# Eight-expert MoE behind an FFT filter: weight halves written once to DRAM, scales from sums of squares, float16 from a later group

## The chip, the core and the metric

The kernel runs on one core of a Trainium2 chip. The time is the device time of one execution, in microseconds (us); three executions of the kernel before give a median of 2247.62 us (2238.39 to 2249.82).

## What is computed

A filter in the frequency domain over the 2496 positions of 8 batches, and then a mixture of experts: each of the 19968 rows goes to the two of 8 experts with the highest noisy logits.

```python
X = np.fft.rfft(x, axis=1)                      # x: 8 x 2496 x 256
y = np.fft.irfft(X * (filt_r + 1j * filt_i), n=2496, axis=1)
x = y.reshape(19968, 256)
noisy = x @ w_gate + np.log1p(np.exp(x @ w_noise)) * noise
top2 = np.argpartition(-noisy, 2, axis=1)[:, :2]      # weights: softmax over the two
for e in range(8):
    for k in range(2):
        mask = top2[:, k] == e
        out[mask] += top2_w[mask, k, None] * (np.maximum(x[mask] @ w1[e], 0) @ w2[e])
# w1: 8 x 256 x 1024, w2: 8 x 1024 x 256
```

## The kernel before

**Two streams, one order.** `fft_stream` (L611) yields the filter step by step: short Fourier transforms as matmuls (`s1`, `kgl` to `kg2`, `t3`, `i2`), rows `y` written to DRAM with their gate values, then gating and routing of a finished batch, which fill `tabs` (the expert of each block) and `lst` (its rows). `expert` (L1242) is a second stream, over blocks of up to 512 routed rows of one expert. `run` (L1315) interleaves the two: a block yields 13 times, and after each yield `run` takes as many filter steps as `PACE` allows for the group. A scheduler then sets the order within each engine from the written program, save where `pin` holds a step at its place.

**Blocks.** They come in groups by how many batches are routed ("ready"). With ready 1 to 3 there are 2, 10 and 6 single blocks of 512 rows. From ready 4 to 8 two blocks of one expert share its weights: 3 pairs with ready 4, then four groups of 5 pairs. Behind them stand the rows left over: 7 single blocks of 512, 14 units of 256 rows and 4 of 128, and more units in a branch (`tc.If`) that the data of this run don't need.

**One block.** POOL gathers the rows (`gather`, L1079), a DMA transposes them (`flip`, L1118) and `turn` splits them into a high and a low half. `front` (L1056) loads the weights (`load_w`, L1186) and splits them (`wsplit`, L1212), 4 pieces of w1 and 4 of w2, one ACT instruction for the high half and one DVE instruction for the low half each. Every product is made of three matmuls, high by high, high by low and low by high (`_mm3`, L123; its matmuls have the lines 124 to 126 wherever it is called from `expert`). A block has 8 `hps` tiles of 6 matmuls, 48 of 128x512, each tile followed by ACT's Relu `hh` (L1278) and DVE's `hl` (L1279), and 96 `yps` matmuls of 128x256. ACT scales `yps` by the gate into `stage` (L1305), POOL adds it to `out` in DRAM (L1306).

**Two number formats.** With `ready < HALF` the halves are float32 of reduced mantissa (in the rows: f32). With `ready >= HALF`, here 4, they are float16 (f16), scaled by powers of two: for the rows by the greatest |y| of the batches (`ymax`, a DVE reduction of each filter output in `i2`, L544), for the weights by the greatest |w| of each expert. The latter is found by `wscales` (L582): 64 loads `wp` of 256 KB on SP's queue, 64 DVE reductions (L593), then `powers` and the table `wtab` (L608). It is a generator, `self.preps`, whose next step is written at every second `write()`, a call that each filter step of the later batches makes. At the first block with `ready >= HALF`, `gather` writes all steps that are left, and then POOL copies the block's scales into `sc` (L1090).

**Weights of the units.** A block or pair of 512 rows loads its 8 pieces into slots of `stage`. A unit loads w1 as 1 MB into `wb` (tag G) and w2 by turns into `stage` slots or into `wc`. Every unit splits what it has loaded. `fetch` keeps two blocks ahead, of which one may stand transposed.

## Time and profile before

| | |
|---|---|
| median of 3 runs | 2247.62 us |
| the profiled execution, by its own time | 2256.64 us |
| its span in the profile | 2254.8 us |
| mean granted TensorE clock | 0.982 |
| PE busy | 2132.7 us (95%) |
| DVE busy | 1594.0 us (71%) |
| ACT busy | 1327.7 us (59%) |
| POOL busy | 1040.2 us (46%) |
| DMA | 392.37 MB, mean 174 GB/s |

PE is TensorE's matmuls, PEld its weight loads, which run beside them; DVE, ACT and POOL are VectorE, ScalarE and GpSimd, SP is the engine that only issues DMAs. A row of a group of instructions reads: line, engine, operation, out<-in by the program's names, partitions x elements and type, count, busy time and mean time of one in ns, and behind the last bar the idle time ahead of them with what ended it. The mean of a matmul is from its start to its end, and these overlap; the pace of a row of matmuls is read from their starts.

### The profile page before, as it was taken

The numbers are of one execution on the slowest core, as the hardware profiler recorded it, in microseconds if no ns is written. First come the engines' busy times: TensorE is split into PE (matmuls) and PEld (weight loads), VectorE is DVE, ScalarE is ACT, GpSimd is POOL, SyncE is SP. The second block draws the span as 40 slices with busy tenths as digits, with TensorE's granted clock in tenths as the row PEclk, the third lists the DMA queues.
The fourth block names the chain that finished last, engine by engine and source line by source line (L and its number), as shares of the span: only waits on it lengthen the run. The fifth ranks groups of instructions, "written<-read, shape, count | busy, mean of one in ns | idle before, by whom it ended". The sixth has DMA issues, their size and how long they took to land. (4 is left out here: it accounts for less than half of the span.)

```text
span 2254.8 us, 43746 instructions
## 1 busy us (share of the span) xinstructions
PE 2132.7 (95%) x14522; PEld 1564.4 (69%) x14522; DVE 1594.0 (71%) x3463; ACT 1327.7 (59%) x2513; POOL 1040.2 (46%) x955
## 2 busy tenths in 40 slices
...
GB/s 239 160 239 174 233 209 176 218 217 215 186 186 200 175 148 179 179 159 157 170 149 152 133 146 131 175 120 132 118 127 136 120 124 141 175 175 245 247 251 146
DMA packets 485871, 392.37 MB, mean 174 GB/s; under 512 B 206251, under 2 KB 387587, under 8 KB 485635
## 3 DMA queue, kind: packets, MB, share of 16 engines
...
q14 instruction: 120, 0.98, 0.2%
...
## 5 line engine op out<-in xcount | busy, mean ns | idle before, releaser
L124 PE MATMUL yps<-w,hh 128*128 128x256 f16 (+1 forms) x2528 | 686.9, 277 | 13.9 <-ACT hh L1278 8.7
L125 PE MATMUL yps<-w,hh 128*128 128x256 f16 (+1 forms) x2528 | 679.9, 276 | 0.1
L126 PE MATMUL yps<-w,hl 128*128 128x256 f16 (+1 forms) x2528 | 670.7, 276 | 7.6 <-DVE hl L1279 6.1
L1306 POOL DMA_INDIRECT out<-stage,ids x316 | 529.5, 1676 | 312.4 <-ACT stage L1305 222.8
L1094 POOL DMA_INDIRECT stage<-y,ids x316 | 352.9, 1117 | 556.7 <-DMA xt<-stage 470.6
L1279 DVE SCALAR_TENSOR_TENSOR hl<-hps,hh 128x512 f16<-128x512 f32 (+3 forms) x712 | 429.2, 621 | 215.1 <-ACT hh L1278 163.6
L124 PE MATMUL hps<-mxh,w1h 128*128 128x512 f16 (+3 forms) x1424 | 497.4, 362 | 18.1 <-DVE hl L1279 13.2
L125 PE MATMUL hps<-mxl,w1h 128*128 128x512 f16 (+3 forms) x1424 | 507.3, 360 | 1.6 <-DVE mxl L1176 1.3
L126 PE MATMUL hps<-mxh,w1l 128*128 128x512 f16 (+3 forms) x1424 | 505.8, 359 | 0.0
L1278 ACT ACTIVATE hh<-hps 128x512 f16<-128x512 f32 (+3 forms) x712 | 373.0, 548 | 143.5 <-PE hps L126 135.7
L1305 ACT ACTIVATE stage<-yps,gt 128x256 f32<-128x256 f32 x316 | 143.6, 476 | 327.4 <-PE yps L126 167.7
L124 PEld LDWEIGHTS <-hh 128*128 128x128 f16 x1952 | 191.2, 98 | 63.7 <-ACT hh L1278 7.8
L126 PEld LDWEIGHTS <-hl 128*128 128x128 f16 x1952 | 190.3, 98 | 63.6 <-DVE hl L1279 13.4
L125 PEld LDWEIGHTS <-hh 128*128 128x128 f16 x1952 | 191.2, 98 | 43.2 <-issue 6.0
L126 PEld LDWEIGHTS <-w1l 128*128 128x128 f16 x1136 | 111.4, 98 | 100.3 <-issue 1.2
L125 PEld LDWEIGHTS <-w1h 128*128 128x128 f16 x1136 | 111.5, 98 | 87.9 <-issue 17.9
L124 PEld LDWEIGHTS <-w1h 128*128 128x128 f16 x1136 | 111.4, 98 | 71.1 <-issue 7.4
L1134 DVE SCALAR_TENSOR_TENSOR w1l<-stage,sc,w1h 128x512 f16<-128x512 f32 x120 | 88.8, 744 | 77.3 <-ACT w1h L1133 50.6
L540 ACT COPY yt<-q 117x1024 uint16<-117x1024 uint16 x96 | 90.6, 944 | 52.5 <-PE q L534 41.9
L1228 DVE SCALAR_TENSOR_TENSOR w<-stage,sc,w 128x512 f16<-128x512 f32 x156 | 111.9, 744 | 9.3 <-ACT w L1227 3.8
L124 PEld LDWEIGHTS yps<-w,hh 128*128 128x128 f32 x576 | 110.3, 192 | 11.2 <-ACT hh L1278 4.1
L1133 ACT ACTIVATE w1h<-stage,sc 128x512 f16<-128x512 f32 x120 | 86.0, 719 | 50.0 <-PE hps L125 29.3
...
## 6 DMA issues: line engine op xcount, KB each, us to landing
...
```

The lines of the kernel that those rows point to most:

```text
L124: nc.tensor.matmul(o, lh, rh, start=start, stop=False)
L125: nc.tensor.matmul(o, lh, rl, start=False, stop=False)
L126: nc.tensor.matmul(o, ll, rh, start=False, stop=stop)
L540: e = nc.scalar.copy(yt.bitcast(U16)[:, :k, :256].rearrange("p g (two d) -> p g two d", two=2), p.bitcast(U16)[:RP, :2 * m].rearrange("p ( ...
L1094: self.pin(lambda: nc.gpsimd.indirect_dma_start(out=x.bitcast(I32), out_offset=None, in_=self.y[:BLK + ready * ROWS], in_offset=bass.Indir ...
L1133: self.nc.scalar.activation(h, x, AF.Copy, scale=s)
L1134: self.nc.vector.scalar_tensor_tensor(l, x, s, h, op0=ALU.mult, op1=ALU.subtract)
L1228: nc.vector.scalar_tensor_tensor(l, sv, sc[:, 1], h, op0=ALU.mult, op1=ALU.subtract)
L1278: nc.scalar.activation(h, p, AF.Relu)
L1279: v = nc.vector.scalar_tensor_tensor(l, p, 0.0, hf[0], op0=ALU.max, op1=ALU.subtract)
L1305: nc.scalar.activation(o, p, AF.Copy, scale=gate[:, t])
L1306: a = nc.gpsimd.indirect_dma_start(out=self.io["out"][:BLK + ready * ROWS], out_offset=bass.IndirectOffsetOnAxis(ap=ids[:, t:t + 1], axis= ...
```

## The change

1. `HALF` goes from 4 to 5: the 3 pairs with ready 4 keep reduced float32.
2. `wscales` takes the sum of squares of each weight row instead of its greatest value, by ACT's Square with an accumulated output; DVE keeps one small reduction for every four. Loads run three ahead of their use. A step is written at every 4th `write()`, and `powers` takes half the exponent, since its input is squared. `TX` and `TW1` are moved to suit.
3. `i2` leaves out the `ymax` reduction for the first two batches (24 instructions). Instead the finished rows of these are read again from DRAM later, 12 loads and 12 reductions.
4. Once the scales are done and the last batch is routed, `wscales` goes on, one step at every third yield of `expert`: it loads each expert's w1 and w2 (16 loads of 1 MB), splits them into float16 halves (64 ACT and 64 DVE instructions, in the buffers `fr` and `fi` of the filter, whose use is over) and writes them to `wpl` in DRAM (16 writes of 1 MB).
5. The 7 singles and all units load these halves (`load_planes`, 2 loads of 1 MB) into three sets of buffers by turns and split nothing: 200 ACT and 200 DVE instructions of these 25 blocks are gone. Units load when they are gathered, two blocks ahead; two of them may stand transposed; the list of rows of a unit is read one unit earlier. Once the last batch's rows are written, `hh` and `hl` of every block are pinned at their place.

**PE behind the 18th block.** `yps` and `hps` are matmuls of blocks; L407 to L409 (`kg1`), L341 to L343 (`s1`), L508 and L510 (`t3`), L532 to L534 (`i2`) and L446 are the filter's. Before, the end of block 18 and what follows it:

```order
L126 MATMUL yps<-w_9857,hl 128x256
L407 MATMUL q_7323<-th,hl 128x512
L408 MATMUL q_7323<-tl,hl 128x512
L409 MATMUL q_7323<-th,hl 128x512
L341 MATMUL q_7354<-xh,hl 120x512
L342 MATMUL q_7354<-xh,hl 120x512
L343 MATMUL q_7354<-xl,hl 120x512
L532 MATMUL q_7439<-th,hl 117x512
L533 MATMUL q_7439<-tl,hl 117x512
L534 MATMUL q_7439<-th,hl 117x512
L508 MATMUL q_7535<-ident,G 120x128 x4
```

This is the start of 106 filter matmuls with no matmul of a block among them. After, the same end:

```order
L126 MATMUL yps<-w_9774,hl 128x256
L446 MATMUL q_7862<-cf,a 128x2x64 x4
L124 MATMUL yps<-w_9830,hh 128x256
L510 MATMUL q_7919<-ident,G 120x128 x4
L125 MATMUL yps<-w_9830,hh 128x256
L126 MATMUL yps<-w_9830,hl 128x256
L124 MATMUL yps<-w_9830,hh 128x256
L125 MATMUL yps<-w_9830,hh 128x256
L126 MATMUL yps<-w_9830,hl 128x256
L124 MATMUL hps<-mxh_9868,w1h 128x512
L125 MATMUL hps<-mxl_9869,w1h 128x512
L126 MATMUL hps<-mxh_9868,w1l 128x512
```

The first block with ready 4 now stands some rows behind the end of the 18th; from there to the 22nd block the longest run of filter matmuls is 28, and from the 29th to the 50th block the two orders are equal.

**DVE at the first single block.** `hl` is the low half of `hps`, L1134 (after: L1202) splits rows and, before, weights as well; L627 is the new split of `wscales`. Before:

```order
L1279 SCALAR_TENSOR_TENSOR hl<-hps,hh 128x512 x2
L1158 COPY stage<-xt 128x2x512 x2
L1279 SCALAR_TENSOR_TENSOR hl<-hps,hh 128x512 x2
L1134 SCALAR_TENSOR_TENSOR mxl_23721<-stage,xs_20041,mxh_23720 128x512
L1279 SCALAR_TENSOR_TENSOR hl<-hps,hh 128x512
L1134 SCALAR_TENSOR_TENSOR mxl_23725<-stage,xs_20041,mxh_23724 128x512
L1134 SCALAR_TENSOR_TENSOR w1l<-stage,sc,w1h 128x512
L1279 SCALAR_TENSOR_TENSOR hl<-hps,hh 128x512 x3
L1134 SCALAR_TENSOR_TENSOR w1l<-stage,sc,w1h 128x512
L1279 SCALAR_TENSOR_TENSOR hl<-hps,hh 128x512 x2
```

After:

```order
L1370 SCALAR_TENSOR_TENSOR hl<-hps,hh 128x512 x2
L1226 COPY stage<-xt 128x2x512 x2
L627 SCALAR_TENSOR_TENSOR fi<-fr,wtab,fi 128x512
L1370 SCALAR_TENSOR_TENSOR hl<-hps,hh 128x512 x2
L1202 SCALAR_TENSOR_TENSOR mxl_23861<-stage,xs_20026,mxh_23860 128x512
L1370 SCALAR_TENSOR_TENSOR hl<-hps,hh 128x512
L627 SCALAR_TENSOR_TENSOR fi<-fr,wtab,fi 128x512
L1202 SCALAR_TENSOR_TENSOR mxl_23865<-stage,xs_20026,mxh_23864 128x512
L627 SCALAR_TENSOR_TENSOR fi<-fr,wtab,fi 128x512
L1370 SCALAR_TENSOR_TENSOR hl<-hps,hh 128x512
L627 SCALAR_TENSOR_TENSOR fi<-fr,wtab,fi 128x512
L1370 SCALAR_TENSOR_TENSOR hl<-hps,hh 128x512 x4
```

The last splits of `wscales` stand between the `hl` of the last pair. On SP's queue the last write to `wpl` stands between the first single's load of w1 halves and that of its w2 halves.

**ACT in a unit of 256 rows.** `hh` is the Relu, `mxh` the high half of the rows, `stage<-yps` the output; `w1h` is a weight split. Before:

```order
L1133 ACTIVATE w1h<-wb,sc 128x512
L1278 ACTIVATE hh<-hps 128x256 x2
L1133 ACTIVATE w1h<-wb,sc 128x512
L1278 ACTIVATE hh<-hps 128x256 x2
L1133 ACTIVATE mxh_27203<-stage,xs_20041 128x256
L1133 ACTIVATE w1h<-wb,sc 128x512
L1278 ACTIVATE hh<-hps 128x256
L1133 ACTIVATE mxh_27207<-stage,xs_20041 128x256
L1305 ACTIVATE stage<-yps,gt 128x256
L1133 ACTIVATE w1h<-wb,sc 128x512
L1278 ACTIVATE hh<-hps 128x256 x2
```

After:

```order
L1369 ACTIVATE hh<-hps 128x256 x4
L1201 ACTIVATE mxh_26762<-stage,xs_20026 128x256
L1369 ACTIVATE hh<-hps 128x256
L1201 ACTIVATE mxh_26766<-stage,xs_20026 128x256
L1396 ACTIVATE stage<-yps,gt 128x256
L1369 ACTIVATE hh<-hps 128x256 x3
L1396 ACTIVATE stage<-yps,gt 128x256
```

Weight splits stood between the Relus of a unit before; after, only the rows' splits and the outputs do.

The diff, cut to its core:

```diff
@@ -134,12 +134,13 @@
 RAW = 3
-HALF = 4
-PLANES = 6
+HALF = 5
+STEP = 4
+EVERY = 3
 FIRSTS = 2
-TX, TW1, TW2 = 3, 2, 14
+TX, TW1, TW2 = 1, 4, 14
 TINY = 2.0 ** -60
@@ -541,14 +543,15 @@
             self.yev.append(e)
-        nc.vector.tensor_reduce(self.ymax[:RP, n, g0 // 4:g0 // 4 + 1], yt.bitcast(U16)[:, :k, 128:256].bitcast(BF16),
-                                axis=AX.XY, op=ALU.max, apply_absolute_value=True)
+        if n >= 2 * FIRSTS:
+            nc.vector.tensor_reduce(self.ymax[:RP, n, g0 // 4:g0 // 4 + 1], yt.bitcast(U16)[:, :k, 128:256].bitcast(BF16),
+                                    axis=AX.XY, op=ALU.max, apply_absolute_value=True)
         if h:
...
-    def powers(self, m, n, t):
+    def powers(self, m, n, t, squared=False):
@@ -558,6 +561,9 @@
         v.tensor_single_scalar(e, a.bitcast(I32), 23, op=ALU.arith_shift_right)
+        if squared:
+            v.tensor_scalar_add(e, e, 127.0)
+            v.tensor_single_scalar(e, e, 1, op=ALU.arith_shift_right)
         v.tensor_scalar(s[:, 0:1], e, -1.0, float(254 + t), op0=ALU.mult, op1=ALU.add)
@@ -585,28 +591,75 @@
         def load(i):
-            t = self.P.tile([128, 512], F32, name="wp", tag="tl", bufs=3)
+            t = self.P.tile([128, 512], F32, name="wp", tag=("tl", "th")[i % 2], bufs=3)
             nc.sync.dma_start(t, io["w1" if i < 4 * E else "w2"][i // 4 % E, i % 4])
         def top(i, t):
-            v.tensor_reduce(self.wquart[:, i % 4:i % 4 + 1], t, axis=AX.X, op=ALU.max, apply_absolute_value=True)
+            nc.scalar.activation(t, t, AF.Square, accum_out=self.wquart[:, i % 4:i % 4 + 1])
             if i % 4 == 3:
-        for i in range(8 * E):
-            t = self.pin(load, i, hold=False)
-            yield
-            self.pin(top, i, t, hold=False)
-            yield
+        Y = [(bt, h, g) for bt in range(FIRSTS) for h in range(2) for g in range(0, NG, 8)]
+        def load_y(i):
+            bt, h, g = Y[i]
+            t = self.P.tile([128, 8, 64], I32, name="wp", tag=("tl", "th")[i % 2], bufs=3)
+            y = self.y[BLK + bt * ROWS:BLK + (bt + 1) * ROWS].rearrange("(p g) d -> p g d", p=RP)
+            k = min(8, NG - g)
+            nc.sync.dma_start(t[:RP, :k], y[:, g:g + k, 128 * h + 64:128 * h + 128])
+            return t[:RP, :k].rearrange("p g w -> p (g w)").bitcast(BF16)
+        def top_y(i, t):
+            bt, h, g = Y[i]
+            v.tensor_reduce(self.ymax[:RP, 2 * bt + h, g // 8:g // 8 + 1], t, axis=AX.X, op=ALU.max, apply_absolute_value=True)
+        raw, cut = (t.rearrange("p h k d -> p (h k d)")[:, :4096].rearrange("p (s q f) -> p s q f", s=2, q=4) for t in (self.fr, self.fi))
+        def load_all(i):
+            nc.sync.dma_start(raw[:, i % 2], io["w1" if i < E else "w2"][i % E].rearrange("q p f -> p q f"))
+        def split(i, q):
+            a, e = i // E, i % E
+            o = cut[:, i % 2].rearrange("p q f -> p (q f)").bitcast(F16).rearrange("p (q f) -> p q f", q=4)
+            h, l, t = o[:, q, :512], o[:, q, 512:], raw[:, i % 2, q]
+            nc.scalar.activation(h, t, AF.Copy, scale=self.wtab[:, a, e:e + 1])
+            v.scalar_tensor_tensor(l, t, self.wtab[:, a, e:e + 1], h, op0=ALU.mult, op1=ALU.subtract)
+            if q == 3:
+                nc.sync.dma_start(self.wpl[e, a].rearrange("q p f -> p q f"), o)
+        def pairs(first, then, n):
+            old = []
+            for i in range(n + 3):
+                if i >= 3:
+                    self.pin(then, *old.pop(0), hold=False)
+                if i < n:
+                    old.append((i, self.pin(first, i, hold=False)))
+                yield
+        yield from pairs(load, top, 8 * E)
         for a, t in enumerate((TW1, TW2)):
-            q = yield from self.powers(self.wmax[:, a * E:a * E + E], E, t)
+            q = yield from self.powers(self.wmax[:, a * E:a * E + E], E, t, True)
             v.tensor_copy(self.wtab[:, a], q[:, 0])
...
             yield
+        yield from pairs(load_y, top_y, len(Y))
+        self.scaled = True
+        yield
+        self.pin(load_all, 0)
+        yield
+        for i in range(2 * E):
+            if i + 1 < 2 * E:
+                self.pin(load_all, i + 1)
+            yield
+            for q in range(4):
+                self.pin(split, i, q)
+                if q < 3:
+                    yield
@@ -740,7 +793,7 @@
             count[0] += 1
-            if count[0] % 2 == 0:
+            if count[0] % STEP == 0 and not self.scaled:
                 next(self.preps, None)
@@ -1058,16 +1111,20 @@
         lt, n, nt, s, tabi, ready = ent[0]
-        with self.after(self.spw):
-            re = nc.sync.value_load(tabi[0:1, 1, s:s + 1], min_val=0, max_val=E - 1)
-        w1st = self.load_w(re, "w1", nt)
-        w1 = []
         sc = ent[2][3]
-        for q in range(4):
-            with self.after(self.yev.pop(0) if self.yev else None):
-                w1.append(self.wsplit(w1st[q], "w1", sc))
-        self.yev = []
-        w2st = self.load_w(re, "w2", nt)
+        if self.tail(tabi):
+            w = ent[2][4]
+            w1, w2st = self.load_planes(tabi, s, w) if isinstance(w, int) else w
+        else:
+            with self.after(self.spw):
+                re = nc.sync.value_load(tabi[0:1, 1, s:s + 1], min_val=0, max_val=E - 1)
+            w1st = self.load_w(re, "w1", nt)
+            w1 = []
+            for q in range(4):
+                with self.after(self.yev.pop(0) if self.yev else None):
+                    w1.append(self.wsplit(w1st[q], "w1", sc))
+            self.yev = []
+            w2st = self.load_w(re, "w2", nt)
         if fill:
@@ -1084,10 +1141,15 @@
             if ready >= HALF:
-                for _ in self.preps:
-                    pass
+                while not self.scaled:
+                    next(self.preps)
                 self.sc = self.P.tile([128, 3, 1], F32, name="sc", bufs=3)
                 nc.gpsimd.tensor_copy(self.sc, self.wtab[:, :, bass.ds(self.ra, 1)])
+        w = None
+        if self.tail(tabi):
+            w = self.wodd = (self.wodd + 1) % 3
+            if nt < BLK // 128:
+                w = self.load_planes(tabi, s, w)
         xg = []
@@ -1096,7 +1158,10 @@
             xg.append(x)
-        return xg, self.turns["xg"] + 1 - nt, self.ra, self.sc
+        return xg, self.turns["xg"] + 1 - nt, self.ra, self.sc, w
+    def tail(self, tabi):
+        return any(tabi is t for t in self.tabs[NB:])
@@ -1119,10 +1184,13 @@
         ent = next((e for e in self.ahead if not e[3]), None)
-        if ent is None or not self.by_dma(ent) or self.standing:
+        if ent is None or not self.by_dma(ent) or self.standing > (len(ent[2][0]) < 4):
             return
-        self.standing = True
-        xt = self.P.tile([128, 4, 512], U16, name="xt", bufs=1)
+        self.standing += 1
+        if len(ent[2][0]) < 4:
+            xt = self.P.tile([128, 4, 256], U16, name="xt", tag="a", bufs=2)
+        else:
+            xt = self.P.tile([128, 4, 512], U16, name="xt", bufs=1)
         for t, x in enumerate(ent[2][0]):
@@ -1176,12 +1244,32 @@
         if ent[3]:
-            self.standing = False
+            self.standing -= 1
         else:
...
+    def load_planes(self, tabi, s, k):
+        nc = self.nc
+        for _ in self.preps:
+            pass
+        with self.after(self.spw):
+            re = nc.sync.value_load(tabi[0:1, 1, s:s + 1], min_val=0, max_val=E - 1)
+        if k < 2:
+            t = (self.fr, self.fi)[k].rearrange("p h k d -> p (h k d)")
+            w = [t[:, 2048 * a:2048 * a + 2048] for a in range(2)]
+        else:
+            w = [self.P.tile([128, 2048], F32, name="wb", tag="G", bufs=2) for _ in range(2)]
+        res = []
+        for a, t in enumerate(w):
+            t = t.bitcast(F16)
+            self.spw = nc.sync.dma_start(t.rearrange("p (q f) -> p q f", q=4), self.wpl[bass.ds(re, 1), a].rearrange("e q p f -> p (e q) f"))
+            res.append([t[:, 1024 * q:1024 * q + 1024].rearrange("p (a b c) -> p a b c", a=2, b=2) for q in range(4)])
+        return [(t[:, 0], t[:, 1]) for t in res[0]], res[1]
@@ -1211,6 +1299,8 @@
         nc, P = self.nc, self.P
+        if len(st.shape) == 4:
+            return st
         if nm == "w2":
@@ -1275,8 +1365,9 @@
                     hf = f32v(h),
-                nc.scalar.activation(h, p, AF.Relu)
-                v = nc.vector.scalar_tensor_tensor(l, p, 0.0, hf[0], op0=ALU.max, op1=ALU.subtract)
+                hold = lambda g: self.pin(g) if self.rows == NB - 1 else g()
+                hold(lambda: nc.scalar.activation(h, p, AF.Relu))
+                v = hold(lambda: nc.vector.scalar_tensor_tensor(l, p, 0.0, hf[0], op0=ALU.max, op1=ALU.subtract))
                 if f == 4:
@@ -1352,9 +1444,11 @@
                          for i, (u, n, _) in enumerate(ENDS)]
-            for i, (u, n, _) in enumerate(ENDS):
-                for s in range(n):
-                    yield from cut(self.read_list(NB + 1 + i, s, u), NB)
+            it = (self.read_list(NB + 1 + i, s, u) for i, (u, n, _) in enumerate(ENDS) for s in range(n))
+            soon = [next(it)]
+            while soon:
+                soon += [b for b in (next(it, None),) if b]
+                yield from cut(soon.pop(0), NB)
@@ -1373,6 +1467,10 @@
                 pass
+            if state["ready"] >= NB - 1:
+                state["k"] += 1
+                if state["k"] % EVERY == 0:
+                    next(self.preps, None)
         with self.tc.If(self.more[0] + self.more[1] < sum(E * CAPB * BLK // u for u, _, _ in ENDS)):
```

## Rows read from the trace of the kernel before

**Rows 1.** Windows: length, busy (xcount) PE PEld DVE ACT POOL, clock, DMA, GB/s

```profile
60.00:190.00 130.00, 100.59 (x474) 59.50 (x473) 100.12 (x341) 77.79 (x139) 28.91 (x27) 0.88 0.67 198
190.00:735.00 545.00, 515.29 (x3257) 446.10 (x3256) 423.32 (x892) 324.50 (x619) 221.84 (x180) 0.98 0.82 202
735.00:790.00 55.00, 39.57 (x195) 26.43 (x193) 35.94 (x79) 32.27 (x58) 14.51 (x15) 0.84 0.66 179
790.00:1580.00 790.00, 782.20 (x5468) 534.00 (x5469) 593.02 (x1352) 468.85 (x860) 380.41 (x340) 1.00 0.68 152
1580.00:2042.00 462.00, 459.67 (x3187) 310.67 (x3186) 249.76 (x399) 231.92 (x424) 258.04 (x245) 1.00 0.68 143
2042.00:2208.00 166.00, 155.03 (x1341) 128.70 (x1339) 134.47 (x277) 126.87 (x277) 98.45 (x111) 0.99 0.93 247
2208.00:2246.00 38.00, 29.66 (x317) 23.56 (x315) 30.38 (x75) 29.13 (x75) 13.09 (x12) 0.96 0.61 148
```

**Rows 2.** Waits, whole span: who, for what; us, times, longest

```profile
DVE wquart L593 <- DMA wp<-w: 64.8, 36, 5.8
POOL sc L1090 <- DVE wtab L608: 31.5, 1, 31.5
...
ACT yt L547 <- DVE ymax L544: 12.8, 15, 1.9
```

**Rows 3.** Timeline of DVE, 735 to 790: start, us, instruction, idle

```profile
768.30 0.69 DVE L593 TENSOR_REDUCE wquart<-wp 128x1 f32<-128x512 f32 x1 [1.82 <-DMA wp<-w]
...
783.03 0.16 DVE L608 TENSOR_TENSOR wtab<-wtab,xm 128x8 f32<-128x8 f32 x1
```

**Rows 4.** Groups of instructions by shape, whole span

```profile
L593 DVE TENSOR_REDUCE wquart<-wp 128x1 f32<-128x512 f32 x64 | 43.5, 682 | 69.8 <-DMA wp<-w 64.8 <-issue 5.0
L544 DVE TENSOR_REDUCE ymax<-yt 117x1 f32<-117x512 bf16 x80 | 54.2, 677 | 18.6 <-ACT yt L540 15.8 <-issue 2.5
L1133 ACT ACTIVATE w1h<-wb,sc 128x512 f16<-128x512 f32 x72 | 51.7, 718 | 13.7 <-PE hps L126 7.3 <-DMA wb<-w 4.5 <-PE hps L125 1.1
L1228 DVE SCALAR_TENSOR_TENSOR w<-stage,sc,w 128x512 f16<-128x512 f32 x156 | 111.9, 744 | 9.3 <-ACT w L1227 3.8 <-issue 2.9 <-PE hps L125 1.9
L124 PEld LDWEIGHTS yps<-w,hh 128*128 128x128 f32 x576 | 110.3, 192 | 11.2 <-ACT hh L1278 4.1 <-DVE hl L1279 2.0 <-ACT mxh L1133 0.6
L124 PEld LDWEIGHTS <-hh 128*128 128x128 f16 x1952 | 191.2, 98 | 63.7 <-ACT hh L1278 7.8 <-issue 6.1 <-ACT w1h L1133 1.9
```

**Rows 5.** Timeline of PE, reduced float32: start, us, instruction

```profile
607.67 0.29 PE L124 MATMUL yps<-w,hh 128*128 128x256 f32 x1
...
609.71 0.28 PE L126 MATMUL yps<-w,hl 128*128 128x256 f32 x1
...
616.68 0.39 PE L124 MATMUL hps<-mxh,w1h 128*128 128x512 f32 x1
...
618.06 0.39 PE L124 MATMUL hps<-mxh,w1h 128*128 128x512 f32 x1
```

**Rows 6.** Timeline of PE, float16

```profile
1704.17 0.38 PE L124 MATMUL hps<-mxh,w1h 128*128 128x512 f16 x1
...
1704.82 0.38 PE L124 MATMUL hps<-mxh,w1h 128*128 128x512 f16 x1
...
1706.33 0.27 PE L124 MATMUL yps<-w,hh 128*128 128x256 f16 x1
...
1708.30 0.27 PE L124 MATMUL yps<-w,hh 128*128 128x256 f16 x1
```

**Rows 7.** Timeline of PE, first matmul of 256-row and 128-row units

```profile
2038.18 0.27 PE L124 MATMUL hps<-mxh,w1h 128*128 128x256 f16 x1
...
2207.92 0.22 PE L124 MATMUL hps<-mxh,w1h 128*128 128x128 f16 x1
```

**Rows 8.** DMA queues, 2080 to 2200: packets, MB, share of 16 engines

```profile
q1 hardware_dynamic: 24056, 23.92, 69.4%
q0 software_dynamic: 3776, 5.08, 21.4%
```

10 lines of the change are left out of this document (6 added, 4 removed).

## The prediction

> **What bounds the kernel now.** I read the windows first, then the waits and the timeline where a window shows a loss, then the durations by shape. The windows [rows 1] show four kinds of stretch. From 790 to 2042 PE is busy 782.20 of 790 us and 459.67 of 462 us at a granted clock of 1.00: there the end is set by the matmuls, and work taken off another engine gives nothing. From 60 to 190 PE is busy 100.59 of 130 us, DVE is busy for about as long. From 735 to 790 PE is busy 39.57 of 55 us at a clock of 0.84. From 2042 to 2246, the units, DMA stands at 0.93, and DVE and ACT are at 134.47 and 126.87 of 166 us, the highest shares that both have in one window. So there are three places in which time can be had: the start (29 us idle on PE), the hole (15 us idle, and slow matmuls besides), and the units. The stretch from 190 to 735 has 30 us of idle PE in 545.
>
> **The change part by part.** All sums stand against the profiled execution, 2256.64 us (1.84 us of it outside the span). It is 9.0 us above the median of the three runs, so I take 9 off at the end.
>
> (a) *The `ymax` reductions of the first two batches.* 24 of them go, at 677 ns [rows 4] 16.2 us of DVE. ACT's copy waited for them for 12.8 us in 15 places in the whole span [rows 2]. If every such wait held PE, that would be the gain, but ACT is not busy throughout there (77.79 of 130 us); and where DVE has other work queued the 16 us only come earlier. I take **-6** of 0 to -10. The 12 re-reads and their 12 reductions come where PE is full or nearly so; their 8 us of DVE lie beside it.
>
> (b) *The scales.* DVE loses 64 reductions, 43.5 us [rows 4], and the 64.8 us in which it stood at `wquart` waiting for `wp` [rows 2], as each load stood one step ahead of its use. What was queued behind such a wait is `hl`, which PE's `yps` need. ACT gets 64 Squares. The trace has none; the nearest row is ACT's scaled copy of 128x512 at 718 ns [rows 4], so 46 us more in a stretch where ACT is busy 324.50 of 545 us [rows 1]. With three loads ahead ACT should not stand for `wp`. PE idles only 30 us in this stretch, so the gain can't be more than some of that: **-4**, from -12 to +6 (the loss if every eighth Square holds PE for its 0.7 us).
>
> (c) *The hole.* POOL's `sc` waited 31.5 us for `wtab` in one place [rows 2]. The timeline shows why [rows 3]: a `wquart` still stood for its load at 768.30, and `wtab` was written at 783.03. All gathers of the first float16 pair are queued behind `sc` on POOL, so PE had nothing but the filter's 106 matmuls, which then run dry. Of 55 us PE was busy 39.57 at a clock of 0.84 [rows 1], which is 39.57 x 0.84 = 33 us of work at full clock: 22 us are lost. After, the three pairs with ready 4 need no scales, and the order shows their matmuls right behind the 18th block. `wtab` is due one group on. By the written order it is step 71 of `wscales`; 70 steps stand ahead of the first block with ready 4 and 80 of 87 ahead of the first pair with ready 5, and between the two lie six blocks, 6 x 22.6 = 136 us by the pace under (d). I take **-20**, from -10 (half moves) to -22. What is late next, if it is late, is the same `sc` one group on (a rival).
>
> (d) *Six blocks in reduced float32.* The pace is read from starts. In float32 18 starts of `yps` from 607.67 to 609.71 span 17 gaps, 0.120 us each, and `hps` goes 6 matmuls from 616.68 to 618.06, 0.230 us [rows 5]. In float16 `yps` goes 18 matmuls in 1.97 us, 0.1094, and `hps` 3 in 0.65, 0.217 [rows 6]. A block so costs 48 x 0.0133 + 96 x 0.0106 = 1.65 to 1.75 us more, and six of them **+10.5**. This is certain in kind, since the stretch they lie in is PE's; the bounds are 9 and 12. The splits are as many in both forms.
>
> The rows show another difference: a weight load of `yps` takes 192 ns in f32 and 98 ns in f16 [rows 4], and yet the starts in [rows 5] stand 0.120 us apart, so loads overlap and don't set the pace. The Trainium skill (TensorE: Matmul & The Clock Gate, Weight-path perf modes — Fast Weight Load (FWL) and DoubleRow, and Back-to-back issue gap) says that the fast weight load is not for FP32, and that load and matmul together set the spacing of a stream. Taken as a sum of exposed loads that would be 96 x (0.192 - 0.120) x 6 = 41 us more for the six blocks, and the forecast would be next to no change; the starts in this trace speak against it, and I give it no chance.
>
> (e) *The splits of `wscales`.* 64 on ACT and 64 on DVE, at 0.718 and 0.744 us [rows 4] 46 and 48 us, and 32 MB of DMA (16 loads, 16 writes of 1 MB), in about 15 blocks of some 21 us ahead of the first single, so between about 1580 and 1900. Their cover: in the 462 us from 1580 DVE is busy 249.76 and ACT 231.92 us, with DMA at 0.68 [rows 1]. 48 us more in 315 is 15% more for each, which leaves them at 65 to 70%. Behind a split on ACT stands an `hh`, and on DVE an `hl`; PE has two or three `hps` banks ahead of it, one matmul tile being 6 x 0.217 = 1.3 us, longer than one split. On SP's queue a write of halves waits for its fourth DVE split, and behind it stand that queue's loads, rows and transposes; the write of the last expert stands between the two loads of the first single. I take **+4**, from 0 to +20 (the 94 us of both engines at a fifth).
>
> (f) *The 256-row units.* The first matmul stands at 2038.18, that of the 128-row units at 2207.92 [rows 7]: 169.7 us for 14 units, 12.1 each. PE's own work is 96 matmuls of 256 columns at 0.1094 [rows 6], 10.5 us a unit, 147 in all, so 22.7 us are lost. No weight load ends a long wait there; ACT and DVE do, in turn, with w1's splits between the Relus as the order shows. A unit loses 8 splits of 0.72 on ACT and 8 of 0.744 on DVE, 6 us each, and both engines fall from about 80% to half that. What is late next is the DMA: the bytes of the units stay as they are, 2 MB each, and a share of 0.93 over 166 us [rows 1] is 154 us of a full queue, of which 69.4 of the 91% are the loads and transposes on SP's queue [rows 8]. Three sets and units loaded when gathered let the stream start under the singles, where DMA has a third free, and run without gaps. 169.7 - 154 = 15.7 is what DMA allows if nothing is drawn ahead, 22.7 what PE allows: **-14**, from -5 to -22.
>
> On DMA the row shows 247 GB/s at a share of 0.93 [rows 1], hence little room. The Trainium skill (DMA: Bandwidth & Descriptors, Bandwidth) has 1 MB loads at 341 GB/s. By that figure, as an estimate, the 166 us of traffic would take 166 x 247 / 341 = 120 us, PE alone would bind, and the term would be -22 and not -14. I keep the share, since it is what the trace has; no run here shows the page's rate.
>
> (g) *The 128-row units.* Four, from 2207.92 to about 2245, 37 us, of which PE is busy 29.66 at 0.96 [rows 1]. The pieces are the same as in (f), but the splits weigh twice as much against half the matmuls. The end itself (output, last accumulate) stays. **-7**, from -3 to -8.
>
> The sum is -6 - 4 - 20 + 10.5 + 4 - 14 - 7 = **-36.5**: 2220 for the profiled execution, 2211 against the median.
>
> **The rivals.**
> *DMA binds (R2).* A load and a write of 1 MB stand in 12 yields, 12/13 of a block or 19.4 us, which is 108 GB/s more on the 143 GB/s of that stretch: 251, about what the units show at a share of 0.93 [rows 1]. At 143 GB/s for 0.68 a full queue would move only 210. Then loads come late for the last pairs and for the first single, (e) becomes +15, and since the bytes of the units are the same, (f) with (g) shrink to -5. Sum -9.5, 2238. For it: these shares. Against it: each 1 MB load stands a block ahead of its first split, and loads end few waits there now.
> *The hole moves (R3).* The scales are late again at ready 5, since a step is now written at every 4th `write()` and not every 2nd. Then (c) is 0 and the rest stays: -16.5, 2231. Against it: the written order leaves 7 steps there, and these are small re-reads.
> *DVE was worth more (R4).* (a) and (b) take nearly half of the early PE idle time of 29 and 30 us, -26 in place of -10. Sum -52.5, 2195. For it: DVE is busy 100.12 of 130 us at the start. Against it: idle PE there also waits for the filter's own chain of ACT and DVE.
> *The splits hold PE (R5, the slower side).* The mechanism is one place, (e): the pins place a split ahead of `hh` and `hl` of a full PE. If each split holds its product for its ACT part and then its DVE part, 0.72 + 0.744, then 64 x 1.47 = 94 in place of 4: +53, 2301. It decides from (36.5 + 4) / 64 = 0.63 us a split on. For it: in PE's full stretch nothing takes a delay up. Against it: these blocks already have 8 such splits of weights each on ACT and DVE, and PE is idle 2.3 us in 462.
>
> **How the numbers follow.** Forecast 0.58; R2 0.19; R3 0.10; R4 0.08; R5 0.05. The forecast's own range, the terms' ends taken half way, is 2197 to 2226. 8 in 10 want R4 whole and most of R2: 2190 to 2241. A measurement of this kernel can tell about 0.5%, 11 us, from no change. Faster by more, below 2236.4, are the forecast, R3 and R4 almost whole and a third of R2: 0.78. Within it lies most of R2, and what of R3 and R5 is milder: 0.16. Slower: R5 and the far end of R2, 0.06.
>
> **What would show it.** (c): no run of the filter without blocks behind the 18th block; `sc` waits under 2 us; clock 1.00 from 735 to 790. If `sc` waits 20 us at the first pair with ready 5, R3 holds. (a), (b): PE idle of 60 to 190 down by 6, waits for `wp` on ACT under 10 us. (d): 0.120 and 0.230 in these six blocks. (e): PE over 98% busy in the 300 us ahead of the first single; if DMA there nears 0.95 and PE waits for `w`, R2; if PE waits for `hl` with a split just ahead of it on DVE, R5. (f): a unit of 256 rows every 11.1 us in place of 12.1; at 11.8 or more the DMA sets the end, with SP's loads as the releaser. What would make it all wrong is a wait that the trace of before doesn't have: the first single standing for the last write to `wpl`, or a Square that is far longer than a copy.

## The result, and the profile after

The changed kernel takes 2187.46 us (median of 4 runs, 2181.09 to 2191.23) against 2248.72 us of the kernel before: a ratio of 0.972, 95% interval 0.966 to 0.978. A second set of runs on another chip gave 0.9695 (0.967 to 0.972). The forecast was 2211 with a range of 2190 to 2241: the direction was right, the gain of 61 us was 24 more than forecast, and the time lies 2.5 us below the range.

The same seven stretches of both programs, cut at the same places of the work: the first Relu of the 1st, 18th, 29th and 64th block (the 64th is the last of the pairs), the first matmul of the 256-row and of the 128-row units, and the end. The columns are those of [rows 1]: start and end, length, busy us (xcount) of PE, PEld, DVE, ACT and POOL, granted clock, DMA share, GB/s. The counts of PE differ by 13 at most, so each stretch holds nearly the same work. The kernel before:

```profile
0.00:174.40 174.40, 137.34 (x677) 83.76 (x678) 113.48 (x349) 107.62 (x192) 52.31 (x54) 0.91 0.74 211
174.40:708.00 533.60, 504.23 (x3193) 436.19 (x3191) 416.59 (x893) 316.60 (x603) 210.00 (x168) 0.98 0.82 200
708.00:1051.30 343.30, 322.55 (x2138) 223.26 (x2139) 260.52 (x598) 205.86 (x378) 144.95 (x131) 0.97 0.72 172
1051.30:1877.90 826.60, 821.99 (x5750) 560.05 (x5748) 537.61 (x1120) 447.77 (x822) 427.98 (x392) 1.00 0.65 139
1877.90:2038.20 160.30, 158.14 (x1085) 105.52 (x1083) 100.07 (x154) 92.29 (x169) 89.11 (x87) 1.00 0.75 170
2038.20:2207.90 169.70, 158.73 (x1374) 132.02 (x1372) 135.28 (x279) 128.33 (x280) 101.22 (x113) 0.99 0.94 247
2207.90:2254.80 46.90, 29.76 (x318) 23.65 (x316) 30.46 (x76) 29.23 (x75) 14.65 (x13) 0.90 0.53 125
```

The changed kernel:

```profile
0.00:168.10 168.10, 134.78 (x690) 82.94 (x691) 107.98 (x342) 108.69 (x193) 52.23 (x54) 0.93 0.79 221
168.10:681.70 513.60, 497.30 (x3192) 434.19 (x3191) 389.00 (x833) 352.73 (x722) 209.55 (x172) 0.99 0.89 214
681.70:1010.50 328.80, 320.77 (x2131) 258.11 (x2130) 259.67 (x580) 204.66 (x385) 135.78 (x119) 0.99 0.78 176
1010.50:1838.00 827.50, 820.72 (x5738) 558.68 (x5736) 577.91 (x1181) 483.84 (x884) 441.81 (x392) 1.00 0.79 178
1838.00:1997.40 159.40, 158.61 (x1091) 106.33 (x1089) 62.34 (x97) 58.69 (x110) 86.75 (x93) 1.00 0.78 195
1997.40:2147.30 149.90, 149.90 (x1373) 133.64 (x1372) 64.25 (x167) 65.27 (x170) 86.70 (x107) 1.00 1.03 263
2147.30:2189.40 42.10, 25.47 (x317) 22.63 (x315) 12.18 (x46) 12.56 (x45) 11.79 (x12) 0.87 0.60 142
```

Both kernels were profiled a second time (runs before_again and after_again below). With the mean of the two profiles of each:

| stretch | before | after | difference | forecast by its terms |
|---|---|---|---|---|
| start to 1st block | 174.2 | 167.6 | -6.7 | (a) and (b): -10 |
| 1st to 18th block | 535.2 | 514.5 | -20.7 | for both rows together |
| 18th to 29th block | 342.5 | 328.9 | -13.6 | (c) and (d): -9.5 |
| 29th block to the units | 986.0 | 988.9 | +2.9 | (e): +4 |
| 256-row units | 167.5 | 150.5 | -17.0 | (f): -14 |
| 128-row units and end | 46.9 | 41.9 | -5.0 | (g): -7 |
| span | 2252.2 | 2192.1 | -60.1 | -36.5 |

So 17 of the 24 us that the forecast lacks lie ahead of the 18th block. In the units PE is now busy 149.90 of 149.90 us: nothing is left there but its own matmuls. What was not forecast at all is the end: the last output stage of ACT now ends at 2174.6 and the span at 2189.4, 15 us later, where it was 9 before. The accumulated writes follow one another closely there:

```profile
2169.94 1.59 POOL L1397 DMA_INDIRECT out<-stage,ids  x1 [6.30 <-ACT hh L1369]
2175.61 1.56 POOL L1397 DMA_INDIRECT out<-stage,ids  x1 [4.08 <-ACTq L1474]
2180.16 1.56 POOL L1397 DMA_INDIRECT out<-stage,ids  x1 [2.99 <-DMA out<-stage,ids]
```

The columns are start, length, instruction and, in brackets, the idle time ahead with what ended it. The last write waits 2.99 us for the DMA of the one before it; the wait of the middle one is put down to ACT's branch at L1474, so that the whole is one chain is not shown. The 128-row units now follow one another every 5.8 us and not every 9, which leaves such a chain less cover. By the means of the two profiles, 5.6 of the 10.6 us that these units gain go back.

### The profile page after: what moved, and what is told of

It is laid out like the page before. It is cut to its first block, busy times and chain, and to the rows that moved or that the text cites. A ratio compares the mean times of both kernels' runs of the same rounds, so it can differ in the third digit from the quotient of the medians.

```text
span 2189.4 us, 42880 instructions
## 1 busy us (share of the span) xinstructions
PE 2107.5 (96%) x14517; PEld 1596.5 (73%) x14517; DVE 1473.3 (67%) x3245; ACT 1286.4 (59%) x2505; POOL 1024.6 (47%) x946
## 5 line engine op out<-in xcount | busy, mean ns | idle before, releaser
L1397 POOL DMA_INDIRECT out<-stage,ids x316 | 527.3, 1669 | 339.8 <-ACT stage L1396 245.9
L124 PE MATMUL yps<-w,hh 128*128 128x256 f16 (+1 forms) x2048 | 558.8, 279 | 9.0 <-ACT hh L1369 3.8
L125 PE MATMUL yps<-w,hh 128*128 128x256 f16 (+1 forms) x2048 | 553.2, 277 | 0.0
L126 PE MATMUL yps<-w,hl 128*128 128x256 f16 (+1 forms) x2048 | 543.4, 278 | 6.8 <-DVE hl L1370 6.5
L125 PE MATMUL hps<-mxl,w1h 128*128 128x512 f16 (+1 forms) x1024 | 394.3, 386 | 0.7 <-DVE mxl L1244 0.7
L126 PE MATMUL hps<-mxh,w1l 128*128 128x512 f16 (+1 forms) x1024 | 393.0, 385 | 0.0
L124 PE MATMUL hps<-mxh,w1h 128*128 128x512 f16 (+1 forms) x1024 | 385.5, 388 | 2.7 <-DVE hl L1370 1.7
L126 PEld LDWEIGHTS yps<-w,hl 128*128 128x128 f32 x768 | 145.9, 192 | 15.8 <-DVE hl L1370 8.2
L124 PEld LDWEIGHTS yps<-w,hh 128*128 128x128 f32 x768 | 147.0, 192 | 12.5 <-ACT hh L1369 4.9
L125 PEld LDWEIGHTS yps<-w,hh 128*128 128x128 f32 x768 | 146.6, 192 | 4.4 <-issue 0.6
L126 PEld LDWEIGHTS <-w1l 128*128 128x128 f16 x640 | 62.6, 98 | 71.8 <-issue 1.1
L1226 DVE COPY stage<-xt 128x1024 uint16<-128x1024 uint16 (+2 forms) x174 | 109.8, 685 | 3.0 <-issue 1.9
L125 PEld LDWEIGHTS <-w1h 128*128 128x128 f16 x640 | 62.6, 98 | 54.0 <-issue 4.0
L124 PEld LDWEIGHTS <-w1h 128*128 128x128 f16 x640 | 62.6, 98 | 53.0 <-issue 6.2
```

Source lines behind the costliest of these rows:

```text
L124: nc.tensor.matmul(o, lh, rh, start=start, stop=False)
L125: nc.tensor.matmul(o, lh, rl, start=False, stop=False)
L126: nc.tensor.matmul(o, ll, rh, start=False, stop=stop)
L1226: nc.vector.tensor_copy(xu.rearrange("p (t two) -> p two t", two=2), ent[3][0][:, 2 * kc:2 * kc + 2, :w])
L1397: a = nc.gpsimd.indirect_dma_start(out=self.io["out"][:BLK + ready * ROWS], out_offset=bass.IndirectOffsetOnAxis(ap=ids[:, t:t + 1], axis= ...
```

## The experiments

**The start and the scales.** Undoing one part at a time in the changed kernel, then doing one part alone in the kernel before.

*ymax_kept*

```diff
-        if n >= 2 * FIRSTS:
+        if n >= 0:
             nc.vector.tensor_reduce(self.ymax[...], yt..., op=ALU.max, ...)
...
-        yield from pairs(load_y, top_y, len(Y))
```

> The changed kernel with the ymax reductions of the first two batches left in the filter and without the re-reads. If they are what the first 6 us are: the first block starts at 174 and not at 168, total 2193. If the 6 us come from the order and not from DVE's 16 us there: 168 and 2187. If they also weigh after the first block: over 2195.

2203.30 us, ratio 0.984. Its windows to the 1st and from there to the 18th block:

```profile
0.00:176.00 176.00, 138.50 (x677) 84.36 (x678) 113.33 (x349) 107.36 (x192) 52.42 (x54) 0.89 0.75 209
176.00:701.50 525.50, 502.14 (x3204) 438.50 (x3203) 394.62 (x851) 351.94 (x723) 205.00 (x168) 0.98 0.86 208
```

The 1st block starts 8 us later than in the changed kernel and the 18th 19.8, with 3881 PE instructions done by then in place of 3882. The time is 16 us above the runs of the result, and 22 above one_ahead on the same chip (2181.20, below), whose order up to the 18th block is the changed kernel's; the profiled execution was the longest of the four, 2209.14. So the 24 reductions are worth some 16 to 22 us, as much as their own 16.2 us of DVE or more, and about three times the forecast.

*ymax_after_copy*

```diff
-        if n >= 2 * FIRSTS:
-            nc.vector.tensor_reduce(self.ymax[...], yt..., op=ALU.max, ...)
         if h:
             nc.scalar.copy(yt[:, :k, 128:], self.dense[:, g0:g0 + k])
+        if n >= 0:
+            nc.vector.tensor_reduce(self.ymax[...], yt..., op=ALU.max, ...)
...
-        yield from pairs(load_y, top_y, len(Y))
```

> The run ymax_kept (ymax reductions in the filter for all batches, no re-reads), with ACT's copy of the gate values written ahead of the reduction of the same tile, so that ACT doesn't wait for DVE there. Theory D (DVE is full at the start, and its 16 us cost however they stand): as ymax_kept, first block at 175, 18th at 702, 2203. Theory A (ACT's 12.8 us of waits for ymax cost): first block at 168 to 170, 18th near 684, 2190.

2196.21 us, ratio 0.972, against 2190.15 of the changed kernel on the same chip:

```profile
0.00:170.60 170.60, 136.59 (x690) 82.81 (x691) 116.57 (x364) 108.45 (x194) 52.17 (x54) 0.91 0.78 218
170.60:689.20 518.60, 499.64 (x3201) 434.42 (x3200) 389.15 (x836) 353.03 (x721) 210.63 (x171) 0.99 0.87 212
```

The 18th block stands at 689.2: of the 20 us, 12 go with the exchange of the two lines, and 7 are left with the reductions. Neither theory alone holds. The exchange does two things, though. It takes away a wait of ACT for a reduction that it need not wait for, and it changes the order that the scheduler makes of everything else: of 3879 PE instructions up to the 18th block, at most 3126 stand in one common order in ymax_kept and here, while the changed kernel and this run share 3696 of 3880. So the 7 us are the reductions' in nearly the same order; in the 12 us the wait and the order are not separated.

*before_copy*, in the kernel before

```diff
-        nc.vector.tensor_reduce(self.ymax[...], yt..., op=ALU.max, ...)
         if h:
             nc.scalar.copy(yt[:, :k, 128:], self.dense[:, g0:g0 + k])
+        nc.vector.tensor_reduce(self.ymax[...], yt..., op=ALU.max, ...)
```

> The kernel before with one edit: ACT's copy of the gate values is written ahead of the ymax reduction of the same tile, in all batches. Theory A2 (of the early 26 us some 11 are ACT standing behind ymax): first block at 169 in place of 174, 18th at 697 in place of 708, total 11 less than before if the hole behind the 18th block stays as long. Theory O (the early gain comes from the order that the whole change happens to give): 708 and no change.

2227.13 us against 2238.79, ratio 0.995 (0.993 to 0.997): 11.7 us less, as theory A2 had it.

```profile
0.00:167.00 167.00, 134.73 (x690) 82.16 (x691) 117.44 (x364) 108.61 (x194) 52.83 (x54) 0.94 0.78 222
167.00:694.30 527.30, 499.50 (x3174) 435.66 (x3173) 416.10 (x893) 316.34 (x603) 206.73 (x170) 0.98 0.85 206
```

Two lines changed places, no work was removed, and DVE is as busy as before; the wait of ACT for `ymax`, 12.8 us in [rows 2], is gone. That this wait alone is the 11.7 us is not shown: the order of the engines changed here too (2985 of 3868 PE instructions up to the 18th block stand in a common order with the kernel before), and from 60 to 190 us PE's wait for ACT's `yt` only fell from 10.8 to 9.7 us. Theory O, the order, stays open.

*dve_top*

```diff
-            nc.scalar.activation(t, t, AF.Square, accum_out=self.wquart[:, i % 4:i % 4 + 1])
+            v.tensor_reduce(self.wquart[:, i % 4:i % 4 + 1], t, axis=AX.X, op=ALU.max, apply_absolute_value=True)
...
-            q = yield from self.powers(self.wmax[:, a * E:a * E + E], E, t, True)
+            q = yield from self.powers(self.wmax[:, a * E:a * E + E], E, t)
```

(with `TX`, `TW1` and `TW2` as in the kernel before)

> The changed kernel with the greatest |w| taken by 64 DVE reductions again in place of ACT's Squares; the loads still stand three ahead. The first to the 18th block took 533.6 us before and 513.6 after. Theory W (the 20 us come from loads that stand ahead, so that no engine waits for wp): 514, total as the changed kernel, 2187. Theory D (they come from 43.5 us taken off DVE): 534, total 2207. Half and half: 524.

*one_ahead*

```diff
-            for i in range(n + 3):
-                if i >= 3:
+            for i in range(n + 1):
+                if i >= 1:
```

> The changed kernel with each load one step ahead of its Square, as the loads stood before, and not three. Theory W: ACT now stands for wp as DVE did, some 65 to 100 us in all, the first to the 18th block take 530 to 534 us, total 2203 to 2207. Theory D: 514 and 2187, since DVE has as little to do as in the changed kernel.

The two ran side by side: dve_top 2197.68 us, one_ahead 2181.20. The stretch from the 1st to the 18th block, dve_top first and then one_ahead:

```profile
165.30:688.60 523.30, 500.24 (x3182) 435.09 (x3181) 420.77 (x890) 319.66 (x606) 198.51 (x167) 0.99 0.86 208
```

```profile
164.60:678.50 513.90, 498.73 (x3191) 436.77 (x3190) 390.01 (x833) 352.42 (x721) 205.87 (x172) 0.99 0.88 214
```

Loads that stand one ahead cost nothing (513.9 as in the changed kernel); reductions on DVE cost 9 us there, and 16 between the two medians, of which 5 more lie from the 18th to the 29th block (336.0 against 330.9). In this kernel theory W falls, and D holds for about half of the 20. Nor do loads three ahead keep an engine from waiting for them, as these rows of the waits show for the changed kernel, for dve_top and for one_ahead (us in total, times, longest):

```profile
ACT wp L599 <- DMA wp<-w: 45.7, 29, 4.4
```

```profile
DVE wquart L599 <- DMA wp<-w: 53.8, 34, 4.8
```

```profile
ACT wp L599 <- DMA wp<-w: 49.1, 33, 5.3
```

ACT stands for `wp` 46 to 49 us either way, and the depth of the prefetch changes neither that wait nor the stretch. What these waits cost on ACT is not shown, since no run takes them away. The step that counts in the changed kernel is from one engine to the other.

*before_ahead*, in the kernel before

```diff
-            t = self.P.tile([128, 512], F32, name="wp", tag="tl", bufs=3)
+            t = self.P.tile([128, 512], F32, name="wp", tag=("tl", "th")[i % 2], bufs=3)
...
-        for i in range(8 * E):
-            t = self.pin(load, i, hold=False)
+        old = []
+        for i in range(8 * E + 2):
+            if i < 8 * E:
+                old.append((i, self.pin(load, i, hold=False)))
             yield
-            self.pin(top, i, t, hold=False)
+            if i >= 2:
+                self.pin(top, *old.pop(0), hold=False)
             yield
```

> The kernel before with one edit: its loads of the scales stand two ahead, in two tags by turns; all else, the DVE reductions too, as before. Theory W: the first to the 18th block 514 to 520 in place of 533.6, total some 15 us less than before. Theory D: 533 and no change. If the hole behind block 18 closes as well, since wtab is written earlier, up to 22 more.

2234.08 us against 2241.35, ratio 0.997 (0.995 to 0.999): 7 us less, between the theories. The stretch from the 1st to the 18th block was 524.4 us in its profile (533.6 and 536.8 in the two of the kernel before), and the hole stayed, 84.5 us from the 18th to the 19th block against 79.6. DVE's wait for `wp`, 64.8 us in [rows 2], is shorter:

```profile
DVE wquart L593 <- DMA wp<-w: 52.3, 34, 4.4
```

So with the reductions on DVE, loads that stand further ahead did pay something; one_ahead says only that they don't once ACT does the work.

*ymax3*

```diff
-        if n >= 2 * FIRSTS:
+        if n >= 6:
...
-        Y = [(bt, h, g) for bt in range(FIRSTS) for h in range(2) for g in range(0, NG, 8)]
+        Y = [(bt, h, g) for bt in range(3) for h in range(2) for g in range(0, NG, 8)]
```

> The changed kernel with the third batch's ymax reductions moved to re-reads as well (12 fewer in the filter, 6 more re-reads). By what the first two batches gave, 20 us for 24: up to 10 less, 2178 to 2180. If the third batch's stand where DVE has room: no change, ratio 0.97.

2196.02 us, ratio 0.981, in its profile the 18th block at 680.6: no gain at the start, so what 24 reductions gave there is not a price per reduction. The run is even longer than the changed kernel, and it loses that from the 18th to the 29th block, 339.8 us in place of 328.9:

```profile
680.60:1020.40 339.80, 325.96 (x2121) 260.78 (x2121) 265.81 (x585) 204.26 (x385) 139.84 (x121) 0.97 0.78 176
```

The place where it loses is that of ready 5, which comes up again below.

**The hole and the six float32 blocks.**

*half4*

```diff
-HALF = 5
+HALF = 4
```

> The changed kernel with float16 from ready 4 again, all else as changed. Its order has 116 filter matmuls behind the 18th block without one of a block among them. By the prediction's terms (c) and (d) the hole comes back (+20 to 22) and six blocks get 1.75 us cheaper each (-10.5): some +10, 2197; the 18th to the 29th block 339 in place of 329. Rival (the hole was filled by something else than the late use of the scales): no wait of sc, 2177.

2223.64 us, ratio 0.985; from the 18th to the 29th block 367.3 us:

```profile
682.10:1049.40 367.30, 324.75 (x2132) 226.35 (x2131) 264.43 (x582) 207.82 (x386) 138.63 (x128) 0.93 0.68 158
```

```profile
POOL sc L1147 <- DVE wtab L647: 55.5, 1, 55.5
```

The hole comes back and is wider than before: `sc` waits 55.5 us in place of 31.5, PE has 42 us idle of 367 at a clock of 0.93, and the loss in the stretch is 38 us and not 10. The 18th block comes 26 us earlier than in the kernel before, but `wtab` only 4 us earlier (779 against 783). The loads and Squares are not late: the last Square starts at 730.77, 37 us ahead of the last reduction of the kernel before (768.30 in [rows 3]). But on DVE the steps that make `wtab` for w2 stand behind the gating and routing of a batch (L872 to L1067):

```profile
730.77 0.63 ACT L599 ACTIVATE wp<-wp 128x512 f32<-128x512 f32 x1
...
747.54 0.25 DVE L872 TENSOR_SCALAR rank<-rank 117x176 f32<-117x176 f32 x1
...
772.95 0.27 DVE L561 TENSOR_REDUCE pm<-xm 8x1 f32<-8x128 f32 x1
...
778.95 0.15 DVE L647 TENSOR_TENSOR wtab<-wtab,xm 128x8 f32<-128x8 f32 x1
```

*half4_step3*

```diff
-HALF = 5
-STEP = 4
+HALF = 4
+STEP = 3
```

> float16 from ready 4 as in the run half4, but a step of the scales at every third write() in place of every fourth, so that all of them stand ahead of the first block with ready 4 in the order; no run of filter matmuls over 16 is left there. By the terms (c) and (d): no hole, six blocks cheaper, -10, 2177, less than both kernels. Rival: the Squares and loads, a third denser up to the 18th block, cost what the float16 gives, 2187.

2200.26 us, ratio 0.975: not less than the changed kernel. No wait of `sc` for `wtab` is left, but the stretch takes 333.2 us in float16, against 328.9 in the changed kernel with six blocks in float32. In slices of 10 us, where the first blocks with ready 5 begin:

```profile
880.00:890.00 10.00, 7.81 (x66) 6.92 (x65) 7.00 (x13) 8.26 (x18) 5.85 (x4) 1.00 0.95 253
890.00:900.00 10.00, 5.63 (x27) 4.70 (x29) 5.25 (x14) 4.38 (x8) 4.90 (x6) 0.63 0.97 262
900.00:910.00 10.00, 6.53 (x25) 2.02 (x26) 3.66 (x6) 3.07 (x7) 4.65 (x7) 0.50 0.54 126
```

PE is busy 20 of 30 us, and after it has idled the granted clock goes from 1.00 to 0.50, the lower of its two levels, for the slice that follows. From 888.0 to 907.7 PE runs 54 matmuls with none of a block among them, and the block behind them waits for the split of its rows:

```profile
907.69 1.44 PE L124 MATMUL hps<-mxh,w1h 128*128 128x512 f16 x3 [3.47 <-ACT mxh L1201]
```

In the changed kernel the longest such run at ready 5 is of 42 matmuls and takes 7 us, 891.6 to 898.6. So the hole lies in PE's order itself, where the blocks seem to have caught up with the filter. It took the gain of the float16, together with the denser Squares: 1st to 18th block 519.6, 5 us more than the changed kernel, and 4 more here.

*before_half5*, in the kernel before

```diff
-HALF = 4
+HALF = 5
```

> The kernel before with HALF = 5 alone. By the terms (c) and (d) as predicted: up to the 18th block as before, 708; 18th to 29th block 343 - 20 + 10.5 = 334; total 9 to 10 less than before. If the six float32 blocks cost nothing since PE would wait at ready 5 anyhow, as the run half4_step3 suggests: 323 to 329, total 15 to 20 less. If the hole moves to ready 5 (R3): 353 or more and slower than before.

2242.03 us against 2238.79, ratio 1.002 (1.000 to 1.004): no gain. Its profile has 337.0 us from the 18th to the 29th block, 5.5 under the mean of the kernel before, with 32.3 us from the 18th to the 19th and a new hole later:

```profile
900.00:910.00 10.00, 9.28 (x69) 8.62 (x69) 6.79 (x13) 7.97 (x17) 3.85 (x3) 1.00 0.90 239
910.00:920.00 10.00, 3.16 (x15) 2.46 (x14) 6.82 (x16) 5.27 (x9) 4.97 (x5) 0.71 0.97 270
920.00:930.00 10.00, 8.05 (x34) 3.65 (x34) 2.98 (x6) 3.02 (x6) 6.34 (x9) 0.50 0.67 163
```

```profile
POOL sc L1090 <- DVE tabi L976: 8.9, 1, 8.9
```

So in the kernel before the hole moves to ready 5, as R3 says, but not because of the scales: `sc` waits there for the routing table of the new batch (`tabi`), at 894. That this wait makes the hole is not shown either, since ymax_after_copy has the same wait, 8.4 us, and with 327.1 us the shortest stretch from the 18th to the 29th block. What before_half5 shares with half4_step3 is the order: 54 matmuls without one of a block, from 908.0 to 928.3. In the changed kernel no `sc` waits for `wtab` or `tabi`, so R3 does not hold. PE's losses near there are smaller and come mostly ahead of those 42 matmuls; its longest wait there is for `hl` of DVE, 3.4 us:

```profile
870.00:880.00 10.00, 7.11 (x47) 5.93 (x45) 7.71 (x13) 3.97 (x7) 2.61 (x3) 1.00 0.94 231
880.00:890.00 10.00, 8.35 (x57) 8.05 (x58) 8.27 (x14) 5.22 (x10) 7.25 (x6) 0.83 1.30 167
```

**The units and the splits.**

*own_splits*

```diff
     def tail(self, tabi):
-        return any(tabi is t for t in self.tabs[NB:])
+        return False
...
         self.scaled = True
         yield
+        return
```

> The changed kernel without halves in DRAM: no load, split and write of wscales behind the scales; singles and units load float32 weights at their front and split them as before; the list of rows read one unit earlier and two units standing transposed are kept. Theory S (the units gain by the splits that leave ACT and DVE): 256-row units back to 11.5 to 12.1 us each and not 10.5, 128-row units to 9, total +20 to +30, 2207 to 2217. Theory P (they gain by lists and rows that stand earlier): 10.5 stays, 2187. The stretch with the splits of wscales, 29th to 64th block, is 827 us in both kernels; if the splits cost there, it falls below that.

2211.76 us, ratio 0.980, 18 to 24 us over the changed kernel by the ratios. The 256-row units, and the 128-row units with the end:

```profile
2002.60:2164.40 161.80, 155.93 (x1374) 131.74 (x1372) 133.63 (x279) 126.88 (x280) 106.30 (x111) 1.00 1.02 256
2164.40:2211.00 46.60, 28.51 (x318) 22.40 (x316) 30.22 (x76) 28.89 (x75) 11.89 (x11) 0.95 0.48 118
```

11.6 us a 256-row unit in place of 10.8, and the 128-row units wholly as before: theory S. The singles ahead of the units took 170.9 us here, 10 more than in either kernel, so not all of the 24 us are the units'; no run says why. What is left between 161.8 and the 167.5 of before may be the lists and rows that stand earlier; the two profiles of before differ by 4.5 us there themselves, so it isn't shown. From the 29th to the 64th block this run took 822.5 us; half4 and half4_step3 on the same chip, with all splits, took 824.2 and 826.5. So the splits of `wscales` cost 2 to 4 us. The changed kernel's 827.5 and 828.6 come from other chips, and are no measure: one_ahead and dve_top, with all splits on a third chip, took 822.2 and 820.7, and before_ahead beside them, without any, 820.3.

*planes_at_front*

```diff
-            if nt < BLK // 128:
-                w = self.load_planes(tabi, s, w)
```

> The changed kernel with the units' halves loaded at their front, one block ahead, and not when they are gathered, two ahead. If the third set and the early loads matter since DMA is at 0.93 there: the 256-row units 155 to 162 us in place of 150, the 128-row units over 30 in place of 26, total +8 to +16. If taking the splits off ACT and DVE was all: 150 and 26, no change.

2189.83 us against 2190.15 on the same chip: no change.

```profile
1995.70:2145.30 149.60, 149.60 (x1373) 134.07 (x1371) 63.16 (x167) 65.97 (x170) 91.06 (x107) 1.00 1.05 264
```

Loads one block ahead do as well as two, and PE is busy throughout: the DMA does not bind the units.

*splits_twice*

```diff
             nc.scalar.activation(h, t, AF.Copy, scale=self.wtab[:, a, e:e + 1])
             v.scalar_tensor_tensor(l, t, self.wtab[:, a, e:e + 1], h, op0=ALU.mult, op1=ALU.subtract)
+            nc.scalar.activation(h, t, AF.Copy, scale=self.wtab[:, a, e:e + 1])
+            v.scalar_tensor_tensor(l, t, self.wtab[:, a, e:e + 1], h, op0=ALU.mult, op1=ALU.subtract)
```

> The changed kernel with each of the 64 splits of wscales made twice, on ACT and on DVE, 46 and 48 us more of them behind the 49th block. If their cover is whole, as the first profile says (29th to 64th block 827 us in both kernels): no change, the ratio of the changed kernel. The term (e) as predicted, +4 for 64: +4. Rival R5 (a split holds PE for 1.47 us): +94. The DMA is not doubled.

2194.20 us, ratio 0.970 (0.966 to 0.975) beside 0.9695 (0.967 to 0.972) of the changed kernel, which the intervals don't tell apart; 29th to 64th block 833.9 us, against 828.6 and 826.7 in after_again and planes_at_front on the same chip. 46 us more on ACT and 48 on DVE cost 4 to 7: the cover is nearly whole, and R5 falls.

**The two kernels again.** *after_again* is the changed kernel and *before_again* the kernel before, both without an edit.

> The changed kernel, unchanged, to be compared on one chip with the runs beside it, and profiled a second time. As its first profile: first block at 168, 18th at 682, 29th at 1011, units of 256 rows 150 us in all, last matmul near 2174; ratio 0.972.

> The kernel before, unchanged, profiled a second time, to see how far its stretches vary. If the profiled execution of 2256.6 us is typical: first to 18th block 530 to 537 us, 18th to 19th 78 to 82, the 256-row units about 170. If it was a long one: some 10 us less in one or two of these.

2190.15 us (ratio 0.9695) and 2251.31 us. The stretches of the changed kernel repeat within 2 us from start to the 29th block; those of the kernel before within 4.5, the widest being the 256-row units (169.7 and 165.2) and the 1st to the 18th block (533.6 and 536.8). The runs one_ahead, own_splits, planes_at_front and splits_twice have the changed kernel's order up to the 18th block; with its two profiles they reach that block at 677.9 to 682.4, so a difference of 4 us there is no finding.

**The parts don't add.** Undone one at a time in the changed kernel, the `ymax` reductions, the Squares, `HALF` and the halves in DRAM cost 22, 16, 30 to 36 and 18 to 24 us (the first two beside one_ahead, the others by the ratios): some 90 us in all, where the whole change gave 61. Alone in the kernel before, the exchanged lines gave 12, the loads 7 and `HALF` nothing. What a part is worth here depends on which of the others stand.

## Why the prediction was right and wrong

**(a), the start: mis-sized, -6 for some -16 to -22.** The place and the sign were right. The step that failed is the bound: I took ACT's 12.8 us of waits at half, since "ACT is not busy throughout there", and DVE's 16 us at next to nothing. In ymax_after_copy and before_copy the exchange that ends ACT's waits is worth 12 us each, and the reductions themselves 7 more, so neither could be discounted by the busy share of its engine. Why is argued and not shown: the chain of the filter there runs through ACT and DVE by turns, so a wait on either can stand on the path; but the exchange changes the scheduler's order too. The granted clock adds to it, 0.91 up to the 1st block before and 0.93 after.

**(b), the scales: mis-sized, -4 for some -9, and for half a wrong reason.** I gave the prefetch the lead ("with three loads ahead ACT should not stand for wp"). It does stand for it, 46 us, and one load ahead did as well as three. What paid, 9 us from the 1st to the 18th block, is that neither the waits nor the reductions are on DVE. The limit that I set, the 30 us of idle PE from 190 to 735, was not where it failed: PE's idle time fell from 29.4 to 16.3 us from the 1st to the 18th block, and its busy time by 7 at a clock of 0.99 in place of 0.98. **R4**, to which I gave 0.08, put (a) and (b) at -26; the profiles have -27. Its size was right, and in part by luck. It reckoned with DVE's time alone ("DVE is busy 100.12 of 130 us at the start"), but about 12 of the 27 us go with the exchange of ACT's copy, which leaves DVE as busy as it was; and only 17 of the 27 us are idle time of PE, the rest is matmuls that took less time.

**(c) and (d), the hole and float32: near in sum, -9.5 for -13.6, not in their parts.** The hole behind the 18th block is gone: from the 18th to the 19th block 36.5 us in place of 79.6, and no wait of `sc` for `wtab`. The pace of the six blocks is as the term had it, here 0.120 us a `yps` (801.02 to 802.45, 12 gaps):

```profile
801.02 0.28 PE L125 MATMUL yps<-w,hh 128*128 128x256 f32 x1
...
802.45 0.28 PE L125 MATMUL yps<-w,hh 128*128 128x256 f32 x1
```

The Trainium skill (TensorE: Matmul & The Clock Gate, Weight-path perf modes — Fast Weight Load (FWL) and DoubleRow) has no fast weight load for FP32, and the loads of [rows 4] agree in kind, 192 ns in f32 and 98 in f16. What would have added 41 us is the prediction's further step of taking these loads as exposed; the pace of 0.120 us rules that out, as [rows 5] had it. But half4_step3 shows that float16 there would give nothing back, since PE then idles at ready 5, and before_half5 that the hole moves there: the same line alone, in the kernel before, gave nothing (ratio 1.002) where the terms gave 9 to 10 us. The step that failed is to add the two as if the stretch were PE's throughout; their sum came near only with the other parts of the change in place. PE's order at ready 5 has 54 matmuls without a block in before_half5 and half4_step3 and 42 in the changed kernel. What made the order so isn't settled; the filter running ahead by the 27 us of (a) and (b) would do it, but no run takes this apart.

**(e), the splits: right.** +4 forecast; 2 to 4 on the chip of own_splits, +2.9 in the table for that stretch with the singles, which is within what the stretch varies by from chip to chip.

**(f) and (g), the units: right in kind, 3 us short and 2 over.** The mechanism was splits between the Relus, and own_splits shows it. What failed in (f) is the floor of 154 us for "a full queue": the units take 149.9 us with DMA at 1.03 of its engines, and planes_at_front says that no load is late. So R2 had no ground; in the stretch with the splits the DMA stood at 0.79 with 178 GB/s. (The 0.93 that the prediction reads for 2042 to 2246 holds up to 2208; behind it [rows 1] has 0.61.) The estimate that the prediction made from a figure of the Trainium skill (DMA: Bandwidth & Descriptors, Bandwidth), by which PE alone would bind, came nearer: 263 GB/s were moved and PE was busy throughout, though no run here shows the 341 GB/s that the page gives for 1 MB. In (g) the units gained 10.6 and not 7, and the end gave 5.6 back, which I had taken as fixed: "the end itself stays". It does not: the last writes now end 15 us behind the last output stage and not 9.

The range was too narrow on the fast side because its lower end took R4 alone. R4's -16 and gains in the other terms do not exclude each other: here (c) with (d) gave 4 us more than forecast and (f) with (g) one.
